# Weight casts ahead of the index fetches, five staging slots and TensorE transposes for batch 2 in a fused attention and bilinear-FFN kernel

## The chip, the cores and the metric

The kernel runs on one core of a Trainium2 chip. The metric is the device time of one execution in microseconds (us). Executions of one kernel here scatter by about 0.7% to either side; the medians of the kernel before lie between 397 and 401 us in the rounds of the result (whose chip the record doesn't name) and on the chips 7, 8, 11 and 13, so every ratio below is to runs of the kernel before on the same chip. With one core there is no second die to compare with, and a single run's state can't always be told. Runs over 1.5% above the fastest of their kernel count as slow and are left out of the ratios.

## The reference, cut to what matters

```python
# q, k, v: 8 batches, 8 heads, 576 tokens, 64 per head; 8 global tokens; window 32 to both sides
mask = (abs(i - j) <= 32) | is_global[i] | is_global[j]
attn = softmax(where(mask, q @ k.T / 8, -1e9)) @ v          # per batch and head
x = attn, heads joined                                        # 4608 tokens x 512
out = ((x @ w_a) * (x @ w_b)) @ w_out                         # 512 -> 1536 -> 512
```

## The kernel before

The kernel is a list of operations, each with the engines that may do it, a priority, and the keys that it reads (R) and writes (W, X). A list scheduler with a cost model lays them out in a fixed order for each engine, and semaphores are set from that order. So a priority decides where an operation stands in its engine's order, and the engine executes that order as it is, even if what stands first has to wait. The parts that matter:

```python
NPE = 2        # batches whose K and Q are loaded in contiguous pieces and transposed by TensorE
GPRIO = 12.72  # priority of the indirect fetches of the global tokens' rows
WC = 12.84     # a weight's cast comes so much later in priority than its load
NST = 3        # staging slots for f32 weights
...
def fetch(dst, t, off, idx, key, prio, g, R=()):      # rows of global tokens, by index, on GpSimd
    G.add("POOL", GCOST, lambda e: e.indirect_dma_start(dst, None, src, ...), R=R, W=[key], prio=prio, ...)
...
def load_weight(i, which, prio, after=()):            # 18 weights: 6 of w_b, 6 of w_a, 6 of w_out
    st = xT[:, :, 1160 + 512 * (n % NST) : 1672 + 512 * (n % NST)].bitcast(f32)     # the slot
    G.add("SP", 0.6, lambda e: e.dma_start(st, src), R=after, W=[("wst", n % NST)], prio=prio - 1.0, ...)
    G.add(**edur(WENG, 1024, rate=1), fn=lambda e: cp(e, dst, st), R=[("wst", n % NST)],
          W=keys, prio=prio + WC)                     # WENG is GpSimd alone
...
def cast_v(hb, prio, engs):                           # V to bf16; rows 0 to 7 are the global tokens' V
    G.add(**edur(engs, 256 * n), fn=lambda e: cp(e, dst, src), ...)
    G.add(("DVE", "ACT", "POOL"), ..., lambda e: cp(e, gd, gs.unsqueeze(1).broadcast_to([8, n, 256])),
          R=[("gv8", b % 2, h)], X=keys, prio=prio)   # the small copy vb<-gv
```

The names in the profile: xT is the transposed attention output (its tail serves as weight slots), wa, wb, wo the weights in bf16, vb V in bf16, gv the global tokens' V, grow the fetched rows, eb the exponentials of one unit of attention, HT the hidden layer. TensorE's work comes in attention units (scores, then probabilities times V) and in FFN groups. Groups 0 and 1 hold tokens 0 to 511 and need only batch 0, the later groups wait for later batches.

The softmax here doesn't subtract the row's maximum and nothing guards it: scores larger than these inputs give would overflow.

## Time and profile before

| | before |
|---|---|
| time, median of 3 runs | 397.11 us (397.03 to 399.54) |
| TensorE busy | 369.8 us, 93% of the profiled span of 398.3 |
| GpSimd, VectorE, ScalarE busy | 28%, 50%, 54% |
| the same from 95 to 300 us | TensorE over 98% busy at full clock |

To read it: the kernel is bound by its matmuls from 95 us on, and every us that can be won lies before. For a sum that counts idle time and slow clock together I also charged every matmul with what one of its kind takes in the long full-speed stretch (0.216 us for 512 columns, 0.046 for one of attention's probability matmuls, 0.0165 for one small transpose). I call that sum *work*, and elapsed time minus the work started is what was *lost*. By this account the kernel before has 351.3 us of work and lost 46.9, of which 34.2 were lost before 95 us. This is my own computation from the traces. So the two profiles differ by 3.9 us where the medians differ by 6.1.

### The profile page before, as it was taken

To read this page: it belongs to the slowest core of one execution; us is meant where nothing else is said; L and a number is where in the kernel's file an instruction comes from. 1 tells how busy PE (TensorE), PEld (TensorE's weight loads), DVE (VectorE), ACT (ScalarE), POOL (GpSimd) and SP (SyncE) were. 2 spreads that over 40 slices of the span, in tenths; PEclk is the share of its full clock that TensorE was granted. 3 is DMA by queue.
4 is the path that set the end of the run, shared out by engine and by line. 5 is a ranking of instruction groups with operands and counts; after the bars stand their busy time and mean duration, and the time that the engine had idled before them with its cause. 6 is when DMAs were issued, how large, how long until landed. Compare 5 with 4: busy or idle time off the path is not lost.

```text
span 398.3 us, 7353 instructions
## 1 busy us (share of the span) xinstructions
PE 369.8 (93%) x2864; PEld 180.8 (45%) x2903; DVE 200.9 (50%) x407; ACT 214.9 (54%) x396; POOL 111.3 (28%) x185
## 2 busy tenths in 40 slices
PE   4774979979999999999999999999999999999996
PEld 1442657734444444444444444444444444444442
DVE  4883468753675566555555565555555422322220
ACT  1691768645665767665766666666665323322321
POOL 6887258451312503330342071203000100000000
PEclk9997989989999999999999999999999999999999
DMA  5999989997895595695698679200000001000102
GB/s 195 273 299 242 259 234 258 276 216 194 223 233 135 151 223 127 156 243 134 159 235 168 146 181 218 58 27 28 26 28 26 29 26 52 29 26 28 53 26 107
DMA packets 125442, 57.24 MB, mean 144 GB/s; under 512 B 106367, under 2 KB 115679, under 8 KB 125407
## 3 DMA queue, kind: packets, MB, share of 16 engines
q1 hardware_dynamic: 123199, 56.54, 55.8%
q0 software_dynamic: 1872, 0.21, 0.9%
q8 instruction: 23, 0.38, 0.4%
q14 instruction: 12, 0.10, 0.1%
q10 hardware_dynamic: 336, 0.01, 0.0%
HBM read 40.00 MB, written 9.44 MB: 124 GB/s over the span
## 4 chain that ended last, share of the span: by engine, by line
PE 88%; DVE 3%; POOL 3%; issue 3%; ACT 2%; POOLq 0%; ACTq 0%
PE psum L932 48%; PE psum L969 24%; PE psum L842 8%; PE psum L798 4%; POOL grow L561 2%; PE psum L625 2%; PE psum L729 1%; ACT vb L654 1%; DVE xT L863 0%; DVE kT L500 0%; PE psum L793 0%; POOL vb L655 0%; DVE vb L655 0%; DVE kT L655 0%; POOL kb L655 0%
## 5 line engine op out<-in xcount | busy, mean ns | idle before, releaser
L945 DVE TENSOR_TENSOR HT<-psum,bc 128x512 bf16<-128x512 f32 (+1 forms) x114 | 75.7, 664 | 108.1 <-PE psum L932 104.7
L932 PE MATMUL psum<-xT,wa 128*128 128x512 bf16 (+2 forms) x464 | 113.5, 363 | 6.9 <-POOL wa L655 5.6
L932 PE MATMUL psum<-xT,wb 128*128 128x512 bf16 (+2 forms) x472 | 113.3, 359 | 1.2 <-issue 1.1
L969 PE MATMUL psum<-wo,HT 128*128 128x512 bf16 x418 | 101.0, 383 | 4.0 <-ACT HT L654 2.5
L940 ACT ACTIVATE bc<-psum 128x512 f32<-128x512 f32 (+1 forms) x114 | 65.4, 575 | 40.2 <-PE psum L932 36.7
L826 ACT ACTIVATE eb<-psum 128x960 bf16<-128x960 f32 x64 | 61.3, 970 | 30.0 <-PE psum L798 30.0
L932 PEld LDWEIGHTS psum<-xT,wa 128*128 128x128 bf16 x480 | 44.6, 99 | 51.1 <-POOL wa L655 5.9
L969 PEld LDWEIGHTS psum<-wo,HT 128*128 128x128 bf16 x432 | 40.7, 99 | 51.0 <-ACT HT L654 2.3
L932 PEld LDWEIGHTS psum<-xT,wb 128*128 128x128 bf16 x480 | 42.7, 98 | 43.7 <-issue 2.8
L851 ACT ACTIVATE rec<-psum 128x288 f32<-128x288 f32 x64 | 26.3, 412 | 50.7 <-PE psum L842 50.5
L830 DVE TENSOR_TENSOR eb<-eb,mask 128x960 bf16<-128x960 bf16 x56 | 41.4, 742 | 23.8 <-ACT eb L826 23.7
L863 DVE TENSOR_TENSOR xT<-psum,rec 128x288 bf16<-128x288 f32 (+2 forms) x68 | 41.6, 619 | 7.9 <-ACT rec L857 6.8
L976 ACT ACTIVATE ost<-psum 128x512 f32<-128x512 f32 x36 | 21.5, 598 | 41.6 <-PE psum L969 40.6
L842 PE MATMUL psum<-eb,vb 125*64 125x210 bf16 (+4 forms) x384 | 37.2, 250 | 4.2 <-DVE eb L830 1.7
L842 PE MATMUL psum<-eb,ones 125*64 125x210 bf16 (+4 forms) x384 | 35.5, 242 | 0.0
L842 PEld LDWEIGHTS psum<-eb,vb 125*64 125x64 bf16 (+1 forms) x384 | 21.1, 113 | 26.9 <-issue 13.8
L853 DVE TENSOR_REDUCE gst<-psum 128x16 f32<-128x64 f32 x64 | 14.1, 220 | 35.4 <-ACT rec L851 35.2
L655 POOL COPY qT<-qgT 128x128 bf16<-128x128 bf16 x13 | 4.1, 314 | 88.5 <-PE psum L798 81.6
L857 ACT ACTIVATE rec<-rec 128x288 f32<-128x288 f32 x64 | 27.8, 441 | 1.5
L655 POOL CAST vb<-vs 128x1280 bf16<-128x1280 f32 x13 | 16.7, 1289 | 40.0 <-PE psum L842 32.3
L798 PE MATMUL psum<-qT,kT 64*128 64x210 bf16 (+4 forms) x384 | 25.0, 238 | 1.0 <-DVE kT L655 0.7
L798 PEld LDWEIGHTS psum<-qT,kT 64*128 64x128 bf16 x384 | 11.6, 94 | 25.6 <-issue 15.2
(105 smaller groups left out, 207.1 us busy)
## 6 DMA issues: line engine op xcount, KB each, us to landing
vs<-in_v_dram SPq DMA_DIRECT2D x39, 256.0 KB, 4.3
out_dram<-ost SPq DMA_DIRECT2D x36, 256.0 KB, 2.0
ks<-in_k_dram SPq DMA_DIRECT2D x30, 256.0 KB, 3.7
qf<-in_q_dram SPq DMA_DIRECT2D x24, 288.0 KB, 4.7
xT<-in_moe_w_b_dram SPq DMA_DIRECT2D x6, 512.0 KB, 5.8
xT<-in_moe_w_a_dram SPq DMA_DIRECT2D x6, 512.0 KB, 5.4
xT<-in_moe_w_out_dram SPq DMA_DIRECT2D x6, 512.0 KB, 5.5
ks<-in_k_dram SPq DMA_DIRECT2D x4, 576.0 KB, 8.3
```

What stands on the lines that cost most here:

```text
L798: i = e.matmul(psum[:, ob + hh, s0 : s0 + 10 * w].rearrange("p (j w) -> p j w", j=10), kT[rs][rw, 2 * c + m, :], qT[rs][rw, :, 64 * m + pa ...
L826: G.add("ACT", act_time(2 * SC), lambda e: e.activation(eb[es][:, :, :], psum[:, ob : ob + 2, 0:SC], AF.Exp, scale=0.125), X=keys, W=[("eb ...
L830: G.add("DVE", dve_time(2 * SC, 2) + 0.06, lambda e: e.tensor_tensor(eb[es][:, :, :], eb[es][:, :, :], mask[:, r, :].unsqueeze(1).broadcas ...
L842: i = e.matmul(acc[xs, n, :].rearrange("p (j w) -> p j w", j=10)[:, :, pa - 32 * r : pb - 32 * r], lh, eb[es][0:kk, x, s0 : s0 + 10 * w].r ...
L851: G.add("ACT", act_time(288), lambda e: e.activation(rc[:], acc[:, 1, 0:288], AF.Ln), R=keys[1:], W=[("rec", es)], prio=prio + d[3])
L857: G.add("ACT", act_time(288, False), lambda e: e.activation(rc[:], rc[:], AF.Exp, scale=-1.0), X=[("rec", es)], prio=prio + d[5])
L863: G.add("DVE", 0.06 + nw * 0.0185, lambda e, w0=w0, w1=w1, c0=c0, nw=nw: e.tensor_tensor(xT[:, kc, c0 : c0 + 9 * nw].rearrange("p (w j) -> ...
L932: i = e.matmul(psum[:, bn, n * (f - fc) : n * (f - fc) + n], w[:, kc, 128 * f : 128 * f + 128], xT[:, kc, cols], start=(kc == 0), stop=(kc ...
L940: G.add("ACT", act_time(n * nf), lambda e: e.activation(bc[bi][:, 0 : n * nf], psum[:, bk, 0 : n * nf], AF.Copy), X=[("bank", bk)], W=[("b ...
L945: G.add("DVE", dve_time(n * nf), lambda e: e.tensor_tensor(HT[:, fc : fc + nf, hcol], psum[:, ak, 0 : n * nf].rearrange("p (f n) -> p f n" ...
L969: i = e.matmul(psum[:, ok, :], HT[:, fc, 512 * hs + 128 * tt : 512 * hs + 128 * tt + 128], wo[:, fc, :], start=(fc == 0), stop=(fc == NFC ...
L976: G.add("ACT", act_time(512), lambda e: e.activation(ost[oi][:], psum[:, ok, :], AF.Copy), X=[("bank", ok)], W=[("ost", oi)], prio=prio - 1e4)
```

## The change

The intent: GpSimd should cast each weight as soon as it has landed instead of after six index fetches; five slots should let early weights stream in without waiting for casts; batch 2's K and Q should come in large contiguous pieces, transposed on TensorE, to relieve the DMA queues; and loads and fetches get explicit earliest times and priorities. The diff, cut:

```diff
-    NPE = 2
+    NPE = 3
-    GPRIO = 12.72
-    GVP = 6.07
-    WC = 12.84
+    GPRIO = 40.94
+    GVP = 45.99
+    WC = -5.66
     NST = 3
+    GREL = 27.48
+    K1R, V1R, K2R, V2R, WOR = 28.05, 10.08, 52.88, 68.94, 58.71   (cut: one line each)
+    NEARLY = 10
...
+        if t == "v" and b == 1:
+            after = [("wst", 3), ("wst", 4)]
...
-            R=R, W=[key], group=g, prio=prio, nbytes=0.2)
+            R=R, W=[key], group=g, prio=prio, nbytes=0.2, rel=GREL if prio > 0 else 0.0)
...
-        st = xT[:, :, 1160 + 512 * (n % NST) : 1672 + 512 * (n % NST)].bitcast(f32)
+        si = n % 5 if n < NEARLY else (n - NEARLY) % NST
+        if si < NST:
+            st = xT[:, :, 1160 + 512 * si : 1672 + 512 * si].bitcast(f32)
+        else:
+            st = vs[1][:].rearrange(...)[:, 1024 * (si - NST) : 1024 * (si - NST) + 1024].rearrange(...)
...
-                load_weight(i, "o", WT + 14 * WS + WS * i, [(("v", 1), 0, c) for c in range(5)])
+                load_weight(i, "o", WOT + WS * i)
```

The other differences are some twenty schedule constants (T0, B1, P1, KV1 and so on).

More of the change, by code (lines that the diff above doesn't have):

```diff
@@ L12 @@
     __slots__ = ("engs", "eng", "fn", "durs", "dur", "lat", "prio", "deps", "users", "seq", "start",
-                 "end", "group", "nbytes", "pos", "clock", "need", "val", "name", "ndep", "ready", "bias", "span")
+                 "end", "group", "nbytes", "pos", "clock", "need", "val", "name", "ndep", "ready", "bias", "span", "rel")
 class DmaGroup:
@@ L28, in add @@
     def add(self, eng, dur, fn, R=(), W=(), X=(), prio=0.0, lat=0.2, group=None, nbytes=0, name="",
-            after=(), span=None):
+            after=(), span=None, rel=0.0):
         op = Op()
@@ L34, in add @@
         op.fn, op.lat, op.prio, op.group, op.nbytes, op.name = fn, lat, prio, group, nbytes, name
+        op.rel = rel
         op.seq, op.users, op.need, op.bias, op.span = len(self.ops), [], False, self.bias, span
@@ L92, in schedule @@
         for op in self.ops:
-            op.ndep, op.ready = len(op.deps), op.span[0] if op.span else 0.0
+            op.ndep, op.ready = len(op.deps), op.span[0] if op.span else op.rel
             op.deps = sorted(op.deps, key=lambda d: d.seq)
@@ L378, in build @@
     ENG = {}
-    SEARLY = 5.07
+    SEARLY = 5.52
     NP0 = 4
-    NPE = 2
+    NPE = 3
     EOFF = 1e4
-    GPRIO = 12.72
-    GVP = 6.07
-    WC = 12.84
+    GPRIO = 40.94
+    GVP = 45.99
+    WC = -5.66
     NST = 3
+    GREL = 27.48
+    K1R = 28.05
+    V1R = 10.08
+    K2R = 52.88
+    V2R = 68.94
+    WOR = 58.71
+    WOT = -18.32
+    V1T = 23.44
+    V2T = 31.16
+    K2T = 41.19
+    GA = 6.46
+    NEARLY = 10
     GCOST = 1.2
     LATP, LATA, LATD = 0.3, 0.3, 0.3
-    VLATE = 16.2
+    VLATE = 9.94
     FILL = 26.0
@@ L513, in load_qk @@
                 G.add(engs[0], 0.6, lambda e, dst=dst, src=src: e.dma_start(dst, src), group=g,
-                      W=[(t + "n", h, 0), (t + "n", h, 1)], prio=prio + 0.02 * h, after=after,
+                      rel=(0.0, K1R, K2R)[b], W=[(t + "n", h, 0), (t + "n", h, 1)], prio=prio + 0.02 * h, after=after,
                       nbytes=dma_time(256 * 2304, 2304))
@@ L523, in load_qk @@
                 G.add(engs[m], 0.5, lambda e, dst=dst, src=src: e.dma_start(dst, src), group=g,
+                      rel=K2R if b == 2 else 0.0,
                       W=[(t + "n", h, m)], prio=prio + 0.01 * m + 0.02 * h, after=after,
@@ L537, in load_kv @@
             G.add(eng, 0.5, lambda e, dst=dst, src=src: e.dma_start(dst, src), group=g, after=after,
+                  rel=0.0 if b not in (1, 2) else V1R if b == 1 else K2R if t == "k" else V2R,
                   W=[(vk, h0 // 4 + n, c) for n in range(nh // 4)], prio=prio + 1e-3 * c + pc[c],
@@ L633, in load_weight @@
         g = DmaGroup(f"w{n}")
-        st = xT[:, :, 1160 + 512 * (n % NST) : 1672 + 512 * (n % NST)].bitcast(f32)
+        si = n % 5 if n < NEARLY else (n - NEARLY) % NST
+        if si < NST:
+            st = xT[:, :, 1160 + 512 * si : 1672 + 512 * si].bitcast(f32)
+        else:
+            st = vs[1][:].rearrange("p c h d -> p (c h d)")[:, 1024 * (si - NST) : 1024 * (si - NST) + 1024].rearrange(
+                "p (k w) -> p k w", k=4)
         if which == "o":
@@ L644, in load_weight @@
             keys = [("w" + which, i)]
-        G.add("SP", 0.6, lambda e: e.dma_start(st, src), R=after, W=[("wst", n % NST)], group=g, prio=prio - 1.0,
+        G.add("SP", 0.6, lambda e: e.dma_start(st, src), R=after, W=[("wst", si)], group=g, prio=prio - 1.0,
+              rel=WOR if which == "o" else 0.0,
               nbytes=dma_time(524288, 1024))
-        G.add(**edur(WENG, 1024, rate=1), fn=lambda e: cp(e, dst, st), R=[("wst", n % NST)], W=keys, prio=prio + WC)
+        G.add(**edur(WENG, 1024, rate=1), fn=lambda e: cp(e, dst, st), R=[("wst", si)], W=keys, prio=prio + WC)
     load_weight.n = 0
@@ L981, in ffn_out @@
               prio=prio - 1e4, nbytes=dma_time(262144, 2048), name="store")
-    T0 = 20
-    T2 = 54.29
-    PER = 8.24
-    BIAS = 3.54
-    BIAS1 = 0.75
-    B2 = 37.14
-    S2 = 8.8
-    B1 = 2.12
-    S1 = 4.34
-    WT = -0.51
-    WS = 2.1
-    P1 = 10.18
-    HG = 23.7
-    TL = 19.77
-    VD = 6.68
-    GP = 15.15
-    KMIN = 29.47
-    FC = 1.6
-    CP = 5.88
-    KV1 = 17.76
-    OUT0 = 34.97
+    T0 = 36.16
+    T2 = 54.14
+    PER = 8.46
+    BIAS = 4.34
+    BIAS1 = 0
+    B2 = 37.76
+    S2 = 8.83
+    B1 = 0.27
+    S1 = 5.2
+    WT = -1.5
+    WS = 1.87
+    P1 = 1.85
+    HG = 36.8
+    TL = 22.5
+    VD = 5.99
+    GP = -4.9
+    KMIN = 29.82
+    FC = 1.96
+    CP = 10.36
+    KV1 = 9.0
+    OUT0 = 45.64
     setup_ops()
@@ L1032, in build @@
         if h2 == 0:
-            tl = max(t - TL, KMIN) if b > 1 else KV1
+            tl = max(t - TL, KMIN) if b > 2 else K2T if b == 2 else KV1
             if b < NPE:
@@ L1038, in build @@
             load_qk(("SP", "SP"), "q", b, 0, 8, tl + 0.1)
-            if b >= NPE:
+            if b >= 2:
                 load_g(b, tl + 1.5)
-            load_kv("SP", "v", b, 0, 8, tl + VD)
+            load_kv("SP", "v", b, 0, 8, tl + VD if b > 2 else V2T if b == 2 else V1T)
         if p == NP0:
             for i in range(6):
-                load_weight(i, "o", WT + 14 * WS + WS * i, [(("v", 1), 0, c) for c in range(5)])
+                load_weight(i, "o", WOT + WS * i)
         if h2 == 0 and b < NPE:
@@ L1054, in build @@
         if h2 == 3:
-            globals_(b, t + 2 + PER)
+            globals_(b, t + 2 + PER - GA)
     for fc in range(0, 12, 2):
```

## The prediction

> **What bounds the kernel now.** I read four views in this order: the page, busy times by stretch, the engines in order of time, and the waits of the queue that issues the loads. The slices of the page first (each 9.96 us):
>
> ```profile
> PE   4774979979999999999999999999999999999996
> PEclk9997989989999999999999999999999999999999
> DMA  5999989997895595695698679200000001000102
> ```
>
> From slice 11 on TensorE is 90% busy or more at full clock in every slice but the last: there the kernel is bound by its matmuls, and nothing about loads or casts can shorten it. Everything that can be won lies in the first ten slices, where digits below 9 stand in both rows. The chain that ended last says the same: PE 88%, and next to it "POOL grow L561 2%", the indirect fetches. To size the hole I asked for stretches cut at the events (columns: stretch, its length, then busy us and instructions of PE, PEld, DVE, ACT, POOL; PEclk; DMA share; GB/s):
>
> ```profile
> 20.00:29.98 9.98, 7.46 (x113) 4.21 (x111) 8.03 (x23) 9.19 (x17) 8.70 (x11) 1.00 0.94 301
> 29.98:36.63 6.65, 1.04 (x10) 0.69 (x8) 2.00 (x6) 1.56 (x4) 5.87 (x7) 0.87 1.20 264
> 36.63:42.43 5.80, 5.80 (x32) 2.73 (x32) 1.36 (x2) 1.94 (x2) 2.94 (x3) 0.56 0.79 239
> 42.43:52.20 9.77, 8.83 (x215) 6.72 (x216) 6.66 (x19) 6.52 (x21) 4.13 (x5) 1.00 0.89 237
> 52.20:59.20 7.00, 4.62 (x52) 3.13 (x51) 3.55 (x8) 4.66 (x8) 3.58 (x4) 0.76 0.92 243
> 59.20:80.90 21.70, 21.62 (x244) 15.45 (x242) 16.97 (x36) 16.58 (x33) 13.10 (x13) 1.00 1.09 267
> 80.90:91.50 10.60, 8.10 (x31) 3.42 (x32) 4.70 (x8) 2.90 (x18) 5.23 (x5) 0.84 1.19 220
> 91.50:95.02 3.52, 3.07 (x43) 1.75 (x43) 1.66 (x4) 2.42 (x6) 0.00 (x0) 1.00 0.34 76
> 95.02:300.00 204.98, 201.76 (x1492) 93.03 (x1518) 116.60 (x213) 130.66 (x219) 52.08 (x93) 1.00 0.61 146
> ```
>
> The FFN of tokens 0 to 511 (groups 0 and 1) begins at 29.98 and group 2 at 95.02. In these 65.0 us TensorE is busy 53.1, so 12.0 are idle. Some of the 53.1 is at a reduced clock: 36.63 to 42.43 ran at 0.56, which loses 5.80 x 0.44 = 2.5; at 55.3 a block of 24 probability matmuls and one of 8 FFN matmuls took 1.81 and 1.89 against 1.0 and 1.05 elsewhere, 1.6 lost; from 83.4 31 matmuls of 512 columns took 8.21 where 31 x 0.216 = 6.7 is full rate (0.216 from 24 of them in 5.18 later), 1.5 lost. So some 17.5 us are lost here, in three holes: A around 30 to 42 (5.6 idle + 2.5 slow), B around 52 to 59 (2.4 + 1.6), C around 81 to 91 (2.5 + 1.5); the rest, 1.4, is scattered. Why A: TensorE's and GpSimd's instructions in order of time.
>
> ```profile
> 29.98 1.05 PE L932 MATMUL psum<-xT,wb 128*128 128x256 bf16 x8
> 36.63 1.89 PE L932 MATMUL psum<-xT,wa 128*128 128x256 bf16 x8 [5.61 <-POOL wa L655]
> ...
> 25.98 1.03 POOL L655 CAST wb<-xT 128x1024 bf16<-128x1024 f32 x1
> 27.17 0.97 POOL L561 DMA_INDIRECT grow<-in_q_dram,gidx  x1 [0.16 <-issue]
> ...
> 34.57 0.96 POOL L561 DMA_INDIRECT grow<-in_k_dram,gidx  x1 [0.17 <-issue]
> 35.53 1.05 POOL L655 CAST wa<-xT 128x1024 bf16<-128x1024 f32 x1
> ```
>
> The weights of w_a were issued at 15.7, but their cast stands in GpSimd's order behind six fetches of about 1 us with 0.3 between them and one K cast. That cast frees a staging slot too, so the queue of loads also stops: it waits for casts of wb 9.5 us in three waits, the longest 8.3. B is a chain of V casts and copies (DVE 1.40, ACT 1.27), exp and mask before batch 1's first probabilities; C is the scatter of the hidden columns, eight ACT copies, after group 1's last product, with nothing else ready.
>
> DMA is the other limit of this stage: its share is near 1.0 at 240 to 300 GB/s from 10 to 90 us. So an order only decides what comes first.
>
> **What the Trainium skill says.** "TensorE: Matmul & The Clock Gate", part 1, says that an idle window of about 3.4 us halves the clock and that sustained activity restores it. The trace agrees: after the 5.61 us hole the 8 matmuls took 1.89, against 1.05. So an idle us in A costs about 1.4. "DMA: Bandwidth & Descriptors", specifications, gives 512 B as the least transfer for line rate; a row of K is 256 B, a contiguous piece 2304 B. The trace shows only mixed stretches: 301 GB/s from 20 to 30 us, with large pieces in flight, 239 over the 65 us. "VectorE: DVE Perf Modes", the three transpose paths, has TensorE 390 ns for a 128x128 block and the DMA crossbar 1309; here 36 small transposes on TensorE took 0.76 to 0.94 us, and a transposing DMA lands after 3.1 to 4.2.
>
> **The change part by part.**
> 1. *Casts ahead of fetches.* The weight casts' priority goes from 12.84 after the load's to 5.66 before it, and the ten fetches are held back to 27.5 or later with priorities above 40. GpSimd then casts each weight as it lands. By the queue's times the first three (524 KB each, some 1.9 us at 275 GB/s) are down by 19 to 23, and the casts, 1.04 each, by 25. TensorE finds w_a at 31: 5.6 idle and 2.5 slow go. I leave 0.5. Gain 7.6.
> 2. *Five slots.* Two more of 4 KB a partition lie in V's second buffer. Five loads can be issued from 14.6 on without a cast, and the 8.3 us wait of the queue goes. DMA was busy there anyhow (0.94), so this moves weights ahead of K, Q and V of batch 1, no more. V of batch 1 has to wait for the casts from slots 3 and 4. Bytes: K, Q, V of batch 0 3.7 MB, w_a and w_b 6.3, K and Q of batch 1 2.4, V 1.3: 13.6 MB. The slices of the kernel before reach 13.9 at 55 us. So V lands at about 54, where it was on hand by 40 before, and batch 1's attention begins at about 55 rather than 52. By then TensorE has other work: group 0 is 12 blocks of 8 matmuls at 1.05, group 1 is 24 blocks of 4 at 0.45, 23.4 us together; the second half of batch 0's attention is some 5 and batch 1's transposes 3.1. That is 31 us from 30 on, if the later weights keep up. Hole B (4.0) shrinks; I don't let it go, because the chain from V's landing to the first probabilities (cast 1.4, copy 1.3, exp and mask 1.7) is unchanged: gain 2.
> 3. *Batch 2 by PE.* Removed: four transposing DMAs and 5120 pieces of 256 B, replaced by 512 of 2304 B; four POOL casts become DVE or POOL casts. Added: 144 transposes on TensorE, 8 groups of 18 at 0.38 = 3.1 us, all on the bounding engine, and some 5.6 us of evictions on DVE and ACT (0.45 and 0.56 a piece), which have room (DVE 17.0 and ACT 16.6 of 21.7). Cost 3.1; the DMA relief counts only in that batch 2 is ready sooner. As the banks 4 to 7 are shared with attention, these transposes follow batch 1's last unit.
> 4. *Set order.* Output weights after K and Q of batch 2 (3.1 MB, 19.1 in all, 76 us at 250 GB/s), out-projection of groups 0 and 1 down in priority, batch 2's first attention above it. This gives TensorE 10.4 us of out-projection as filler during batch 2's first units, and something to do while the hidden columns are scattered. Hole C (4.0): gain 2, as wo lands late.
>
> Sum: 7.6 + 2 + 2 - 3.1 = 8.5; less 0.2 for new small waits, 8.3. 397.1 - 8.3 = 388.8 us.
>
> **Rivals.** *(a) The load takes the place of the cast:* GpSimd is free, but the weights come at 2.1 us apiece, and batch 1's V, later than before, opens a hole at 50 to 57. For it: DMA share 1.0 over the whole stage. Against: the sums of point 2 meet within 1 us. Then B stays or grows by 2 and C stays: gain 2 to 4, 393 to 395. *(b) All holes close:* the ceiling. 17.5 less some 2 unavoidable less 3.1 is 12.4: 384.7. For it: the work is there; against: batch 1's attention alone feeds TensorE 1.3 us a unit while ACT needs 1.82 (0.97 + 0.41 + 0.44), so without FFN filler 0.5 a unit is lost, 4 over eight units. *(c) ACT or DVE as bound in 60 to 85* through the added evictions: +1 to 2 us, 390 to 391; their shares of 76 to 78% speak against more. *(d) The steady part gets worse* through the other loads' new places: 98% busy there, and the queue is half idle; I give it little.
>
> **Range and chances.** Between (a) and (b), 384.5 to 393.5 for 8 in 10. The 2% mark is 389.2 and the estimate is 0.4 below it, so it is little better than even: 0.55 faster by over 2%, 0.43 within, 0.02 slower, since hole A can hardly stay.
>
> **What would show it.** Right: no wait of TensorE for a cast of wa at 30 to 37; clock 0.95 or more from 30 to 50; group 2's first 512-column matmul at 85 to 88 instead of 95; 432 transposes of kb and qb instead of 288; ten transposing DMAs of kT and ten of qT instead of twelve each; fetches after 30 us. Wrong: TensorE waiting for a landing of weights or of V between 45 and 60 (rival a), a new hole before batch 2's first probabilities or before the out-projection (wo late), or a stretch after 100 us under 97% busy. If group 2 starts by 83, rival (b) holds.

## The result, and the profile after

The changed kernel takes 403.6 us (median of 4 runs, 401.94 to 403.86), against 397.5 (397.03 to 399.54) for the kernel before in the same rounds: ratio 1.0135, 95% interval 1.0089 to 1.018. Ratios are the mean time of one kernel's fast runs over that of the other's from the same rounds, so not quite the ratio of the medians. The change is no gain of 8.3 us; it is a loss of some 1%, within the 2% mark but outside the range.

The page after, busy tenths in slices of 10.05 us:

```profile
PE   4778899689997999999999999999999999999996
PEclk9787999699999999999999999999999999999999
DMA  5987894999989448949865940300000000100102
```

TensorE's slice 4 (30 to 40 us) has gone from 4 to 8, as hoped. But slices 7 and 8 (60 to 80 us), which read 9 and 9 before, now read 9 and 6, with a clock of 6 in the second, and the DMA's digit in slice 7 has dropped to 4. The clock has also fallen in slices 2 and 3 (from 9 and 9 to 7 and 8), and in slice 4 it reads 7 as before. So one hole closed and others opened.

Equal stretches of both traces (stretch, length, then busy us and instructions of PE, PEld, DVE, ACT, POOL; clock; DMA share; GB/s). Before:

```profile
20.00:30.00 10.00, 7.48 (x113) 4.23 (x112) 8.05 (x23) 9.21 (x17) 8.72 (x11) 1.00 0.94 301
30.00:42.00 12.00, 6.39 (x39) 3.20 (x38) 3.34 (x8) 3.21 (x6) 8.79 (x9) 0.72 1.01 248
...
60.00:72.00 12.00, 12.00 (x141) 8.87 (x138) 9.57 (x19) 9.07 (x19) 9.38 (x9) 1.00 1.12 256
72.00:80.00 8.00, 7.97 (x91) 5.51 (x89) 5.80 (x15) 5.91 (x15) 3.72 (x4) 1.00 1.05 283
80.00:95.00 15.00, 12.01 (x82) 5.51 (x82) 7.19 (x13) 6.19 (x25) 5.23 (x5) 0.89 0.99 191
```

After:

```profile
20.00:30.00 10.00, 7.62 (x92) 3.84 (x88) 8.68 (x13) 6.79 (x13) 6.82 (x10) 0.84 0.84 274
30.00:42.00 12.00, 10.94 (x105) 7.03 (x102) 5.30 (x13) 7.89 (x14) 9.61 (x11) 0.75 0.81 284
...
60.00:72.00 12.00, 10.34 (x116) 7.92 (x114) 10.12 (x22) 8.65 (x17) 5.28 (x6) 1.00 0.56 193
72.00:80.00 8.00, 5.99 (x47) 2.58 (x46) 4.06 (x8) 4.27 (x14) 1.61 (x2) 0.59 0.94 241
80.00:95.00 15.00, 13.10 (x242) 7.60 (x242) 10.68 (x23) 11.09 (x27) 8.34 (x8) 0.99 1.03 265
```

From 30 to 42 TensorE is busy 10.94 instead of 6.39, at a clock hardly better than before (0.75 and 0.72). From 60 to 80 it was busy 19.97 of 20 before, and is 16.33 now. And 5.99 of that ran at a clock of 0.59.

The account of lost us by stretch, before and after, with three of the experiments below, each from its own profiled run (the stretches add up to what was lost, lost and work to the span, but for rounding):

| stretch | before | after | after, copies moved (a2_again) | before, casts first (b1_again) | after, no slots, copies moved (d1_slots3_copies) |
|---|---|---|---|---|---|
| 0 to 20 | 10.6 | 12.0 | 11.5 | 11.5 | 11.5 |
| 20 to 30 | 2.8 | 3.6 | 3.3 | 3.6 | 2.9 |
| 30 to 42 | 8.1 | 3.3 | 0.6 | 4.3 | 2.7 |
| 42 to 66 | 6.9 | 5.2 | 7.4 | 7.4 | 8.6 |
| 66 to 80 | 1.1 | 6.5 | 5.4 | 2.3 | 2.0 |
| 80 to 95 | 4.6 | 2.6 | 2.7 | 3.1 | 0.5 |
| 95 to the end | 12.7 | 15.3 | 15.1 | 13.1 | 14.0 |
| lost | 46.9 | 48.4 | 45.9 | 45.3 | 42.2 |
| work | 351.3 | 353.7 | 353.7 | 351.3 | 353.7 |
| span | 398.3 | 402.1 | 399.6 | 396.7 | 395.9 |

So of the 3.9 us between the two profiled spans 2.4 are more work (the 144 transposes) and 1.5 more loss. Worked out before rounding, hole A gave up 4.9 us, holes B and C 3.7 together, and 10.1 came back elsewhere: 5.4 between 66 and 80, 2.5 after 95 and 2.2 before 30.

**What holds TensorE before 36 us.** VectorE, GpSimd and TensorE of the changed kernel in order of time:

```profile
23.76 3.54 DVE L678 COPY vb<-gv 8x512 bf16<-8x512 bf16 x1
```

```profile
23.27 0.93 POOL L678 COPY vb<-gv 8x512 bf16<-8x512 bf16 x1
24.15 1.03 POOL L678 CAST wb<-xT 128x1024 bf16<-128x1024 f32 x1
25.14 1.03 POOL L678 CAST wa<-xT 128x1024 bf16<-128x1024 f32 x1
26.12 1.03 POOL L678 CAST wb<-xT 128x1024 bf16<-128x1024 f32 x1
```

```profile
28.22 0.58 PE L816 MATMUL psum<-xT,ident 128*128 128x480 bf16 x2 [2.38 <-DVE xT L886]
...
33.56 1.25 PE L955 MATMUL psum<-xT,wb 128*128 128x256 bf16 x5
```

In the kernel before the same copy was this line of VectorE:

```profile
23.26 0.28 DVE L655 COPY vb<-gv 8x512 bf16<-8x512 bf16 x1
```

The copy moves 8 rows and should take 0.28 us. It took 3.54, and it ends at 27.30, right after the last of GpSimd's four back-to-back instructions at 27.15. Everything behind it on VectorE came late, TensorE waited 2.38 us, its clock halved at 29.1, and the first hidden-layer matmul started at 33.56, where it had started at 29.98. So the weights were in time and their user was late. This is the cost of putting casts back to back that I had not seen.

The Trainium skill, "SBUF — State Buffer", section "Who interferes with whom", says that VectorE and GpSimd share one pair of memory ports, which one of them holds for a whole instruction, and that copies and casts of VectorE can need it. It adds that a tensor_tensor with both inputs in SBUF contends with GpSimd's reads and a tensor_reduce never does. The traces agree with all three and add numbers: the copy above; the mask (a tensor_tensor) took 1.56 us against 0.65 during a K cast at 126.75, and TensorE waited 1.88 us for it; and for the tensor_reduce see a8_reduce. The same happened at 46.17 (a copy of 128x32, 2.30 us against 0.11 before). Not every copy is held: the copy of 8x768 at 22.66 ran under a GpSimd cast (22.18 to 23.21) in 0.53 us, as long as in the kernel before.

**What holds it between 66 and 80 us.** The queue that issues the loads in the changed kernel (start, length, kind):

```profile
48.46 4.84 SPq L553 DMA_DIRECT2D vs<-in_v_dram  x5
...
61.09 5.18 SPq L561 DMA_DIRECT2D gv<-grow  x4
66.31 1.55 SPq L667 DMA_DIRECT2D xT<-in_moe_w_out_dram  x3
```

V of batch 1 was issued at 48.46: its buffer was tied to the cast of the tenth weight, which GpSimd reached at 47.40 after fetches and two casts of Q, a wait of 9.4 us. The casts of V and the first small copy then came in this order, in the changed kernel:

```profile
56.77 1.25 POOL L678 CAST vb<-vs 128x1280 bf16<-128x1280 f32 x1 [1.60 <-DMA vs<-in_v_dram]
63.09 1.48 DVE L678 CAST vb<-vs 128x1280 bf16<-128x1280 f32 x1
63.47 1.25 ACT L677 ACTIVATE vb<-gv 8x1280 bf16<-8x1280 bf16 x1
```

and in the kernel before:

```profile
50.22 1.25 POOL L655 CAST vb<-vs 128x1280 bf16<-128x1280 f32 x1
50.25 1.48 DVE L655 CAST vb<-vs 128x1280 bf16<-128x1280 f32 x1
51.76 1.27 ACT L654 ACTIVATE vb<-gv 8x1280 bf16<-8x1280 bf16 x1 [1.16 <-DVE vb L655]
```

Before, the two halves of V were cast side by side. In the changed kernel GpSimd cast one half when V had landed, but the other half stood in VectorE's order behind masks and hidden-layer products; VectorE came to it 6.3 us later and hadn't waited for a landing.

The fetches of the global tokens' V rows, now last in GpSimd's order (48.6 to 55.2), are not what held batch 1. The code fills gv for batches 0 and 1 from PSUM (here at 18.6 and 19.0) and loads it from grow for batches 2 and later only. The four loads at 61.09 are those of batches 2 and 3. The queue stood 4.9 us for the fetches, and behind it stood the output weights; experiment a1 takes these loads out of the way. TensorE:

```profile
65.30 0.27 PE L865 MATMUL psum<-eb,vb 125*64 125x170 bf16 x2
...
71.73 0.27 PE L865 MATMUL psum<-eb,vb 125*64 125x170 bf16 x2 [1.58 <-DVE eb L853]
...
75.77 0.63 PE L992 MATMUL psum<-wo,HT 128*128 128x512 bf16 x1 [1.11 <-POOL wo L678]
```

The first probabilities of batch 1 come at 65.30, 10 us later than before (55.31). By 70 the hidden layer of groups 0 and 1 is used up. My reading, which no experiment tests alone: it should have been the filler between batch 1's units; now the units run alone, TensorE waits for their masks (1.58 and 0.78 us), and the output projection can't help before 75.77.

### The profile page after: what moved, and what is told of

Its sections match the earlier page's. It is cut to its first block, busy times and chain, and to the rows that moved or that the text cites. A ratio compares the mean times of both kernels' runs of the same rounds, so it can differ in the third digit from the quotient of the medians.

```text
span 402.1 us, 7651 instructions
## 1 busy us (share of the span) xinstructions
PE 373.4 (93%) x3005; PEld 184.8 (46%) x3047; DVE 209.6 (52%) x410; ACT 213.9 (53%) x403; POOL 116.2 (29%) x187
## 4 chain that ended last, share of the span: by engine, by line
PE 88%; DVE 6%; issue 2%; DMA 2%; ACT 1%; SPq 0%; POOL 0%
PE psum L955 46%; PE psum L992 24%; PE psum L865 8%; PE psum L821 4%; PE psum L752 2%; DMA xT<-in_moe_w_out_dram 2%; PE psum L642 2%; DVE vb L678 1%; ACT eb L849 1%; DVE eb L853 1%; DVE HT L968 1%; PE psum L816 1%; DVE xT L904 1%; DVE kT L513 0%; DVE xT L886 0%
## 5 line engine op out<-in xcount | busy, mean ns | idle before, releaser
L955 PE MATMUL psum<-xT,wa 128*128 128x512 bf16 (+2 forms) x465 | 110.8, 358 | 1.7 <-issue 0.8
L992 PE MATMUL psum<-wo,HT 128*128 128x512 bf16 x417 | 102.5, 384 | 2.4 <-POOL wo L678 1.1
L865 PE MATMUL psum<-eb,vb 125*64 125x210 bf16 (+4 forms) x384 | 37.5, 253 | 6.3 <-DVE eb L853 5.2
L678 POOL CAST vb<-vs 128x1280 bf16<-128x1280 f32 (+1 forms) x13 | 16.1, 1235 | 47.6 <-PE psum L865 44.5
```

The source lines that it names most:

```text
L678: return e.tensor_copy(dst, src)
L865: i = e.matmul(acc[xs, n, :].rearrange("p (j w) -> p j w", j=10)[:, :, pa - 32 * r : pb - 32 * r], lh, eb[es][0:kk, x, s0 : s0 + 10 * w].r ...
L955: i = e.matmul(psum[:, bn, n * (f - fc) : n * (f - fc) + n], w[:, kc, 128 * f : 128 * f + 128], xT[:, kc, cols], start=(kc == 0), stop=(kc ...
L992: i = e.matmul(psum[:, ok, :], HT[:, fc, 512 * hs + 128 * tt : 512 * hs + 128 * tt + 128], wo[:, fc, :], start=(fc == 0), stop=(fc == NFC ...
```

## The experiments

The engine order was edited after the scheduler had finished, so all else stays in place, except where "scheduler anew" is said. All runs gave the right result. No kernel was refused.

**a0_after, a0_again: the changed kernel unedited.** No edit; yardsticks for the rounds on chips 11 and 8.

> The changed kernel unedited, so that the runs beside it have it on the same chip: ratio 1.005 to 1.018 to the kernel before, as on record (1.0135), with the 8x512 copy of gv on DVE again over 3 us and the first FFN matmul at 33 to 34 us.

> The changed kernel unedited, as the yardstick on this chip. So far it stood at 1.0135 on one chip and 0.9997 on another. Theory (a small loss that the state of the throttle blurs): 1.000 to 1.014. Nothing else is asked of it.

Measured: a0_after 401.52 us, ratio 0.9997 (0.9919 to 1.0075), with runs near 398.6 and near 404; a0_again 404.59 us beside 401.10 before, 1.0099 (1.0055 to 1.0143). So a0_after missed what was expected. The changed kernel is about 1% slower in two of three sets of rounds and not to be told from the kernel before in the third, where its runs fall into two clusters. In both traces the copy took 3.54 us again and the first hidden-layer matmul came at 33.73 and 34.12 (a0_after's trace is of a run at 404.57 us, labelled slow).

**a1_wout_first: the output weights issued before the loads that wait for V's rows.**

```diff
+for op in find(G, "gv2") + find(G, "gv3"):      # four small loads behind the six of w_out
+    before_op(G, op, find(G, "vload2")[0])
```

> Changed kernel, one edit in the queue of loads: four small loads of gathered V rows (gv for batches 2 and 3) go behind the six loads of w_out. Theory 1 (head of the line): the queue stood at gv from 56.2 to 66.3 us, first for the late V fetches, then for batch 1's V copies, and w_out stood behind it; TensorE lost 6.5 us between 66 and 80 by the account of work. Then w_out is issued near 57, its first cast is near 63 instead of 69.9, the loss from 66 to 80 falls to 2 or less, and the time is 398 to 400 against 403.6 (ratio to the kernel before 1.000 to 1.006). Rival: batch 1's attention comes late because V does, TensorE has nothing else to do there either, and out-projection only moves: gain under 1.5 us (ratio over 1.009).

Measured: 401.33 us, 0.998 (0.9903 to 1.0057), 0.2% from the unedited kernel of another round on the same chip. The first cast of w_out came at 65.35 instead of 69.92, and the output projection at 72.34, but time was lost between 66 and 70 all the same: TensorE waited 1.74 and 0.78 us for masks of 1.43 and 1.15 us under those very casts. The late output weights are not the cause of the hole. The run shows one thing more: batch 1's first probabilities came at 61.85, though the four gv loads were issued only at 70.92, so these don't hold batch 1.

**a2_copies_act, a2_again: two small copies move from VectorE to ScalarE** (the copy above and the one at 46.17).

```diff
+op = find(G, "gvcopy01")[0]; before_op(G, op, regs)        # regs: an operation of ScalarE's order
+op = find(G, "xdup")[0];     before_op(G, op, users[0])    # users: who reads it, on ScalarE
```

> Changed kernel, one edit: two small SBUF-to-SBUF copies, the second gv copy of batch 0 (8x512, 3.54 us in the profile of after against 0.28 before) and the copy of eight columns of x (128x32, 2.30 us against 0.11), go from DVE to ACT. Theory 2 (DVE locked out by back-to-back casts on GpSimd): both stalls vanish, DVE's next reductions and products follow at once, the first FFN matmul comes at 30.5 to 31.5 instead of 33.56, and the time falls by 2 to 4 us (ratio 1.004 to 1.009). Rival: the stall is one of the copy's own inputs or of slow clock at the start, or it moves to the next DVE instruction with SBUF operands: first FFN matmul after 33, time within 1 us of 403.6.

> The changed kernel with the two small copies on ScalarE, the same kernel that stood at 0.9926. A later run that held the same edit and three more moved casts stood at 1.0079 on another chip. Theory (the copies held by GpSimd's casts cost the changed kernel some 3 us at the first hidden-layer matmul): 0.989 to 0.998, and at least 0.5% below the unedited changed kernel of the same rounds. Rival (the gain belonged to that chip and its throttle, not to the edit): within 0.4% of the unedited changed kernel.

Measured: 397.96 us, 0.9926 (0.9881 to 0.9971), where a0_after stood at 0.9997 in other rounds on that chip; the first hidden-layer matmul came at 30.42 instead of 33.56. On the later chip it came at 30.92, and the time was 400.24 us, 0.9987 (0.9946 to 1.0027), beside 1.0099 for the unedited kernel of the same rounds. That is 4.35 us less, from 404.59; the rival (an effect of the chip alone) falls, though the ratio lies a little above what I had expected. In the table above the stretch of 30 to 42 us loses 0.6 instead of 3.3. What makes the edit worth less on one chip than on the other is seen in one instruction of VectorE. First trace:

```profile
41.71 0.96 DVE L906 TENSOR_TENSOR xT<-gsb,grc 128x32 bf16<-128x32 f32 x1 [1.02 <-ACT xT L677]
```

Second trace, with GpSimd's instructions of that time:

```profile
43.81 2.61 DVE L906 TENSOR_TENSOR xT<-gsb,grc 128x32 bf16<-128x32 f32 x1 [2.63 <-ACT xT L677]
```

```profile
44.24 1.15 POOL L678 CAST qb<-qf 128x1152 bf16<-128x1152 f32 x1
45.33 1.04 POOL L678 CAST wa<-vs 128x1024 bf16<-128x1024 f32 x1
46.52 0.96 POOL L578 DMA_INDIRECT grow<-in_v_dram,gidx  x1 [0.16 <-issue]
```

The same tensor_tensor of 128x32 (0.18 us when free) came 2.1 us later, met two casts in a row and got through only in the gap before the fetch. TensorE waited 2.1 us for what follows it, and then the clock halved for 6.8 us. So the same order of instructions has cheap and dear executions, by how two engines fall against each other. ScalarE's copy ahead of it (41.45 in the first trace, 43.54 in the second) stands behind a copy of kT that came at 40.28 and at 42.47; what delayed that one I didn't find.

**a3_both: a1 and a2 together.**

> Both edits of a1 and a2 together on the changed kernel. If theory 1 and theory 2 are independent the gains add: 403.6 - 4 - 3 = 396 to 397 (ratio 0.996 to 1.000), as each removes lost TensorE time in another stretch. If the later hole only swallows what the earlier one gives (rival: w_out's landing alone sets the restart at 75), a3 is no better than a1 by more than 1 us.

Measured: 399.18 us, 0.9971 (0.9911 to 1.0031). No better than a2 alone: the order of w_out had nothing to add.

**a8_reduce: the same two copies stay on VectorE, in their place, but as a tensor_reduce over an axis of length one.** This tells whether the copy was held by the shared ports or merely stood in a bad place.

```diff
-cp(e, gd, gs.unsqueeze(1).broadcast_to([8, n, 256]))
+e.tensor_reduce(gd, gs.unsqueeze(1).broadcast_to([8, n, 256]).unsqueeze(3), AxisListType.X, ALU.add)
```

> The lock tested in place. Changed kernel; the same two copies stay on DVE at the same places in its order, but are written as a tensor_reduce over an axis of length one, a form that by the Trainium skill never takes the port pair that DVE shares with GpSimd. Theory 2 (a copy with SBUF source and target waits for GpSimd's casts to pause): the 8x512 copy takes 0.5 to 0.8 us instead of 3.54 and the small one under 0.3 instead of 2.30, with GpSimd's three casts back to back as before; the first FFN matmul comes at 30.5 to 31.5, the time is that of a2 (ratio 0.989 to 1.000). Rival (the data or DVE itself is late, or the casts slow whatever DVE does): the reductions are as long as the copies were, and the ratio stays over 1.005.

Measured: 398.89 us, 0.9952 (0.991 to 0.9994). VectorE, and GpSimd at that time:

```profile
23.59 0.67 DVE L723 TENSOR_REDUCE vb<-gv 8x512 bf16<-8x512 bf16 x1
```

```profile
23.98 1.03 POOL L678 CAST wb<-xT 128x1024 bf16<-128x1024 f32 x1
24.96 1.03 POOL L678 CAST wa<-xT 128x1024 bf16<-128x1024 f32 x1
25.95 1.03 POOL L678 CAST wb<-xT 128x1024 bf16<-128x1024 f32 x1
```

The same bytes at the same place under the same casts: 0.67 us instead of 3.54. The engine, the order and the data are the same, only the kind of instruction differs. That shows that the kind of VectorE instruction decides whether it is held, not its data or its place, which is what the page's account of the shared ports says. The first hidden-layer matmul came at 31.58.

**b1_casts_first, b1_again: part 1 alone, on the kernel before.**

```diff
+first = find(G, "fetch0")[0]
+for n in (1, 2):                                   # the casts of the second and third weight
+    before_op(G, find(G, f"wcast{n}")[0], first)   # go ahead of the six fetches
```

> Kernel before, part 1 of the change alone and nothing else: on GpSimd the casts of the second and third weight go ahead of the six Q and K fetches. My prediction's point 1: the 5.61 us wait of TensorE for the cast of wa and the slow clock after it go, gain 4 to 7 us (390 to 393, ratio 0.983 to 0.990). Rival, as in the changed kernel: three casts back to back hold up DVE copies by 1 to 3 us and the hole moves to the next weights, which wait for staging slots: gain under 3 us (ratio over 0.993).

> The kernel before with only the casts of the second and third weight ahead of the six fetches, the same kernel that stood at 0.9869. The version with one more cast moved stood at 0.9951 on another chip. Theory (part 1 of the change alone is a gain): 0.984 to 0.994. Rival (its gain was within the scatter between chips): 0.995 to 1.002.

Measured: 395.73 us, 0.9869 (0.9809 to 0.9929), and on another chip 396.66 us, 0.9877 (0.9845 to 0.9909), 4.4 us under 401.10. It is the fastest kernel of the study in both rounds. Here the casts run from 25.80 to 28.80, after the copy (0.90 us) is done, and in the first of the two traces nothing of VectorE is held for long. Hole A shrinks from 8.1 to 4.3, and the rest moves on: in the first trace TensorE waits 2.3 us for the fourth weight's cast at 37.5. In the second it waits 1.9 us for VectorE instead, and a cast of Q on VectorE took 2.45 us at 38.01 under two weight casts, against 0.75 just before. So this version isn't free of held instructions either.

**b2_third_too: one cast more.** As b1, and the fourth weight's cast ahead of the last two fetches.

> The kernel before with the casts of the second and third weight ahead of the six fetches (as in the earlier run at 0.9869) and the fourth weight's cast ahead of the last two fetches. In that earlier run TensorE waited 2.3 us for the fourth weight's cast, which stood on GpSimd at 37.5 us behind two fetches and a cast of K. Theory (order on GpSimd): the cast comes at 34 to 35.5 us, that wait falls under 1 us, ratio 0.980 to 0.986. Rival (the weight itself lands near 36 us, so GpSimd stands and waits for the transfer): GpSimd is idle before it, ratio 0.986 to 0.992.

Measured: 398.44 us, 0.9951 (0.9879 to 1.0024). Theory and rival were both too low. The cast came at 34.09 and TensorE's wait for it was gone, but its place was taken by a wait of 2.9 us for a K fetch, now behind that cast. GpSimd is a queue: what one cast gains the next fetch loses. I can't tell this kernel from b1 by its ratio alone, the intervals overlap.

**a4_v_early: V of batch 1 earlier.** The tenth weight's cast, which frees V's buffer, ahead of three fetches and two casts of Q.

```diff
+before_op(G, find(G, "wcast9")[0], find(G, "fetch1")[0])
```

> Changed kernel, one edit on GpSimd: the cast that empties the second slot in V's buffer goes ahead of three K fetches and two casts of Q, so that batch 1's V can be loaded. The queue waited 9.4 us for that cast (39.0 to 48.5). Theory 3 (late V): V's load is issued at 42 to 44, its cast is at 51 to 53 instead of 56.8, batch 1's first probabilities come before 61 instead of 65.3 and more attention runs beside the FFN of groups 0 and 1, gain 2 to 3 us on the changed kernel of the same chip. Rival (what follows from 60 us on is set by the locks between DVE and GpSimd and by w_out): V is early and the gain is under 1 us.

Measured: 407.19 us, 1.017 (1.0124 to 1.0215), worse than the unedited kernel: a miss. The tenth weight itself lands only at 45.2, so GpSimd stood 3.3 us waiting for it, with the fetches and Q casts behind it; V was issued at 46.26, only 2.2 us earlier, GpSimd's cast of it came at 58.79 instead of 56.77, VectorE's at 67.06, and the first probabilities at 69.27 instead of 65.30. The queue's loads of gv ended at 70.2 instead of 66.3.

**a7_v_free: five slots for the first five weights only** (NEARLY 10 to 5; scheduler anew), so V waits for casts near 30 us.

> The changed kernel with five slots for the first five weights only, then three: the two slots in V's second buffer are used once, so V of batch 1 waits for the casts of the fourth and fifth weight (near 30 us) and not for that of the tenth (47.4 us). Scheduler anew. Theory: V's first load then issues before 42 us (48.5 in the changed kernel), its cast comes before 52 us (56.8), the time lost between 66 and 80 us (6.5 us in the changed kernel) falls to 4 or less, and the ratio to the kernel before is 0.990 to 1.002. Rival (the transfers of 30 to 50 us are bound by bandwidth, so an earlier V only pushes weights back): V earlier, weights later, ratio 1.00 to 1.015, as the two other tries to bring V or w_out forward ended.

Measured: 403.92 us, 1.0118 (1.003 to 1.0205). V was issued at 40.13 as expected, but VectorE came to its casts only at 62.55 and 64.87 (expected: before 52), and batch 1's first probabilities came at 65.68. An early issue alone brought nothing; the place of the casts in VectorE's order decides too. The loss of 66 to 80 us fell from 6.5 to 3.7, but by the same account that of 42 to 66 rose from 5.2 to 9.2, so the loss moved and didn't go. The time is the rival's. TensorE waits 2.7 us for the held copy as before and 2.4 more at 43, where a tensor_tensor took 2.24 us under casts; a mask took 3.64 us at 94 and two 1.6 at 127.

**a6_slots3: the five slots undone** (NEARLY 10 to 0; scheduler anew).

> The changed kernel with the five slots undone: three slots for all weights, so V of batch 1 waits for no weight; the scheduler lays the rest out anew with the change's own constants. My prediction gave the five slots 2 us. Theory: the slots are near nought or harmful here, because V's transfer, tied to the cast of the tenth weight, comes late (batch 1's first probabilities at 65.3 us in the changed kernel, 55.3 before): ratio to the kernel before 1.000 to 1.012, first batch-1 probabilities before 60 us. Rival (the slots are what lets the early weight casts run without waiting): GpSimd waits for weights in transfer between 30 and 45 us as it did before, and the ratio is above 1.018. The layout is new, so only a difference of over 1% from the unedited changed kernel (0.9997 to 1.0135 on two chips) counts.

Measured: 400.27 us, 1.0017 (0.995 to 1.0084). Batch 1's first probabilities are at 57.07, GpSimd doesn't wait for weights between 30 and 45, and the loss of 66 to 80 us is 0.95. The theory holds, in that nothing was lost without the slots; by time alone the run can't be told from the unedited kernel, whose ratios lie from 0.9997 to 1.0135. The copy still took 3.54 us and TensorE still waited 2.3 us.

**d1_slots3_copies: no slots, and the two copies on ScalarE.**

> The changed kernel without the five slots (that alone stood at 1.0017) and with the two small copies on ScalarE. In the run without the slots the copy of V's global rows on VectorE took 3.54 us under GpSimd's casts, just as in the changed kernel, and TensorE then waited 2.3 us. Theory: that wait goes and nothing takes its place, ratio 0.990 to 0.997. Rival (the gain is given back at a later wait, as the gain of the two other combined edits was): 0.998 to 1.004.

Measured: 397.84 us, 0.9931 (0.9898 to 0.9964), as the theory said. On that one chip the medians are 404.59 (changed), 400.24 (copies moved), 397.84 (also no slots), with 401.10 before. Stretches of this run:

```profile
60.00:72.00 12.00, 11.97 (x132) 9.52 (x130) 9.73 (x20) 8.45 (x20) 6.62 (x6) 1.00 1.03 298
72.00:80.00 8.00, 7.53 (x188) 5.62 (x186) 6.30 (x16) 6.80 (x22) 3.62 (x4) 1.00 1.00 275
80.00:95.00 15.00, 14.74 (x125) 6.94 (x122) 8.85 (x15) 10.43 (x24) 6.73 (x5) 1.00 0.96 231
```

TensorE is busy 34.24 of the 35 us, at full clock. Batch 1's probabilities start at 54.12, so the hidden layer fills the gaps between its units. What this version loses lies at 42 to 50, where TensorE waits 2.9 us for a K fetch and its clock halves.

**a5_npe2 and d2_npe2: batch 2's Q and K left to the DMA transposes** (NPE 3 to 2; scheduler anew), in the changed kernel and in d1.

> Changed kernel with batch 2's K and Q loaded and transposed by DMA again (one constant, NPE = 2); the scheduler makes its orders anew, so not only this part moves. By the account of work the 144 transposes on TensorE cost 2.4 us of full-rate work; two of the waits for instructions fall beside them. If that part is a net loss: 2 to 4 us faster than the changed kernel beside it. If the contiguous loads pay for it: within 1 us or slower.

> As the run without the slots and with the two copies on ScalarE (0.9931), but with batch 2's Q and K left to the DMA transposes as in the kernel before, scheduler anew. My prediction charged the 144 transposes of batch 2 with 3.1 us of TensorE against what the earlier hidden layer gains; by my account of matmul work they cost 2.4 us. Theory (that part pays its way by work alone, nothing is gained from it): 0.985 to 0.992, that is some 2.4 us below the run with them. Rival (the transposes are worth more than they cost, since batch 2's probabilities come earlier and nothing of the 80 to 95 us hole is left): 0.993 to 1.002.

Measured: a5_npe2 405.81 us, 1.0048 (0.9979 to 1.0118), two of four runs slow: not a gain, no more can be said. d2_npe2 400.94 us over 22 runs, 1.002 (1.0006 to 1.0034), against 0.9931 with the transposes. The theory (undoing them wins their 2.4 us) falls and the rival holds. The loss between 110 and 130 us was 6.3 instead of 2.0, with several waits of 0.8 to 1.4 us for VectorE and GpSimd. A caution: the other constants of the change were made for three batches by TensorE, so this shows that the part pays in this layout, not that it would in every one.

**c1_wo_act: the last three casts of w_out on ScalarE too**, on top of a2's edit.

```diff
+for w, r in zip(late, refs):         # late: the last three casts of w_out; refs: places in ScalarE's order
+    before_op(G, w, r)
```

> The changed kernel with the two small copies on ScalarE (0.9926 in an earlier run) and also the last three casts of w_out on ScalarE in place of GpSimd. In that earlier run a mask on VectorE took 1.47 us against 0.60 while GpSimd cast w_out at 75.1 us, and TensorE waited 1.8 us for it. Theory (VectorE is kept out of the memory by GpSimd's casts): the mask at 75 us takes 0.6 to 0.7 us, the wait falls under 1.2 us, ratio 0.986 to 0.993. Rival: the casts delay ScalarE's exponentials and reciprocals by their own 3 us and give the gain back: ratio 0.993 to 1.000.

Measured: 402.97 us, 1.0079 (1.0013 to 1.0146), above both expectations. Up to 70 us it is the kernel a2, and it fell into a2's dear execution: the tensor_tensor at 44.14 took 2.57 us. The mask was held at 71 us (1.49), now by another of w_out's casts. Since a2 itself was 0.9926 on one chip and 0.9987 on another, c1 says little of its own edit. This run is why a2 and b1 were run again.

## Why the prediction was wrong, point by point

- **What bounds the kernel, and where.** Right. All that the change or the experiments moved lies before 140 us; the steady part was TensorE's in every run.
- **Part 1, casts ahead of fetches: 7.6 predicted.** The mechanism was right and its size wrong, and this is the first step that failed. "5.6 idle and 2.5 slow go. I leave 0.5": TensorE indeed never waits for a cast of wa. But done alone on the kernel before, the part is worth 4.4 to 5.0 us, because the hole moves on to the next cast or fetch. And in the changed kernel its own casts, back to back, held a VectorE copy 3.54 us, so the FFN started 3.6 us later; moving the two held copies to ScalarE (a2) took 4.35 us off the time on one chip. I had costed the casts on GpSimd alone and looked for no one else whom they stop.
- **Part 2, five slots: +2 predicted.** Wrong in sign, the second step that failed. I had V landing at 54, the chain from its landing to the first probabilities unchanged (1.4 + 1.3 + 1.7, some 4.4 us), batch 1's attention at about 55, and 31 us of other work from 30 us on. The count of work was right: TensorE did have work until about 70. The chain is what failed. V was issued at 48.46 and GpSimd's wait for it ended at 56.77, and from there to the first probabilities at 65.30 it took 8.5 us, because half of V waited in VectorE's order until 63.09. By then the work that bridged the time was nearly used up, and it was the filler that batch 1's units need. I had written that argument into rival (b), that attention alone feeds TensorE too little, and didn't apply it here. Undoing the slots, with the schedule anew, gave 2.4 us on one chip. This contains the new layout too; slots and layout weren't separated further. (The bytes of the sum add up to 13.7 MB, not 13.6, which changes nothing.)
- **Part 3, batch 2 by TensorE: cost 3.1.** The work is 2.4 us more, and the profile counts 216 transposes of kb and 216 of qb, with ten transposing DMAs each of kT and qT, as foretold; packets under 512 bytes fell from 106,367 to 96,175. This is about twice the 5,120 pieces of the prediction's sum, which left out the packets of the four transposing DMAs that went. As a net cost it was wrong in the layout tested: undoing it cost d1 0.9%, by their ratios on two chips.
- **Part 4, set order: +2.** The stretch of 80 to 95 us did lose 2.0 less. But 5.4 more were lost at 66 to 80, which is the sign that I had named ("before the out-projection, wo late"). a1 shows that late output weights are not what matters there; d1, in a layout made anew with V early, loses 2.0 there instead of 5.4 (a2_again).
- **Rivals.** (a) had V coming later than before right, but the hole was not at 50 to 57 (42 to 66 lost 1.7 us less); it came at 66 to 80. And it still gave a gain. None of the four allowed for a loss, and the range ended at 393.5 though (a) itself was put at 393 to 395. (b) didn't come. (c) was near the truth in naming VectorE, but through its busy share; what counted was being held. (d) was given little, and 2.5 us were lost there, 2.3 of them at 120 to 130 with the mask held by a K cast.
- **Signs.** Fetches after 30: right. Clock of 0.95 or more from 30 to 50: wrong, 0.85. Group 2 at 85 to 88: wrong, 93.23.

Shown by an experiment: the held copy and its cost, part 1's worth alone, and that late output weights don't make the hole at 66 to 80. Shown for one chip and a layout made anew: 2.4 us less without the slots. Argued from the traces: that the hole at 66 to 80 is filler used up too early. Open: why the unedited changed kernel's runs on chip 11 fall into two clusters, why ScalarE comes 2 us later in some executions of a2, how much of the slots' harm is the slots and how much the order that came with them, and what the transposes are worth under constants made for two batches.

The version that beats both kernels is b1, two moved casts on the kernel before: 0.9869 and 0.9877.

## What to carry to other kernels

When work is moved to GpSimd or packed more densely there, list the VectorE instructions that will run at the same time: here a copy of 8 rows took 3.5 us while GpSimd left no gap, and it was cured by moving it to ScalarE or by another kind of instruction. Filler work is only worth something beside the work whose latency it hides, so ask of a later arrival not whether the engine has something to do meanwhile but what will be left to do afterwards. When data come later, look also where each engine's order puts the casts and copies that follow the landing. A part of a change that is good alone should be run alone: here it was worth 1.2 to 1.3%, and the whole cost 1%.

## What the Trainium skill lacked or had wrong

- "SBUF — State Buffer", section "Who interferes with whom", has the lock and says that the other engine is blocked for the whole instruction. It doesn't say that a waiting VectorE instruction can be passed over again and again: the copy stood through the rest of one GpSimd copy and three casts in a row, 3.54 us against 0.28, and ended 0.15 us after the last. In the traces looked at, VectorE got through when GpSimd paused; that a pause is needed is my reading of three such cases and not tested.
- The same section has no time for a tensor_reduce used as a copy, which is indeed not held: 0.67 us for 8x512 under casts, against 0.28 for a free copy.
- The same section on tensor_tensor with both inputs in SBUF: it agrees, with 2.61 us against 0.18 for 128x32 and 1.56 against 0.65 for 128x960. The first had started 0.43 us before the cast, while GpSimd was issuing an indirect fetch; whether the fetch held it too the trace doesn't tell.
- "TensorE: Matmul & The Clock Gate", part 1, speaks of an idle window of about 3.4 us. Here the clock halved at 29.1 us after a wait of 2.38 us, with TensorE busy 0.78 us of the 3.00 from 26 to 29, and stayed halved for 6.8 us. The page doesn't say how idle a window has to be. Counting only holes over 3.4 us underrates the small ones.
- The same part says that the window is free-running, so that the number of slow matmuls at a kernel's start differs from run to run, and puts this ramp under 1% of a typical span. What halvings later in a kernel cost from run to run it doesn't say. Here the changed kernel's runs on one chip lay at 398.6 to 399.1 us with a mean granted clock of 0.986, and at 404.0 to 404.6 with 0.97, 1.4% apart; whether the clock is the cause or follows from other waits isn't shown.
